# Attention and FFT gate on one core: matmuls in column and row tiles, the output projection one batch later, time in nine blocks

## The chip, the cores and the metric

The program runs on one core of a Trainium2 chip. A core has a matrix engine (PE in the profile, with its weight loads shown as PEld), a vector engine (DVE), a scalar engine (ACT), GpSimd (POOL) and a queue engine (SP). The engines run side by side, each takes its own instructions in order, and semaphores tie them together. Matmul results land in PSUM; everything else lives in SBUF. The metric is the device time of one execution in microseconds (us); the profile's span runs from the first to the last instruction.

## The reference

For 8 batches, 8 heads, 576 time steps and 64 channels per head, a linear attention without softmax is normalised per head, and its output (576 x 512 per batch) goes through a projection, a circular convolution in time, two gates and an output projection:

```python
kv = np.einsum('bhsd,bhse->bhde', k, v)
out = np.einsum('bhsd,bhde->bhse', q, kv)
rms = np.sqrt(np.mean(out * out, axis=-1, keepdims=True) + 1e-06)
x = out / rms * g_norm                      # then heads side by side: (B, 576, 512)
proj = x @ w_proj                           # 512 -> 3 * 512: x1, x2, x3
X2 = np.fft.rfft(x2, n=S, axis=1)
H = np.fft.rfft(filter_fft, n=S, axis=0)[None, :, :]
x2_conv = np.fft.irfft(X2 * H, n=S, axis=1)
y = x1 * x2_conv * x3
out = y @ w_out
```

All inputs and the output are float32 in memory; the kernel converts to bfloat16 as it loads and accumulates in float32.

## The kernel before

Channels lie on the partitions for most of the way (512 channels are four groups of 128, `NDC = 4`), time on the free axis. The Fourier transforms are matmuls with cosine and sine tables. Time is split in three thirds of 192 (`SB`): `fold` forms the sum of the thirds (`rr`) and two differences (`ab`). Frequencies that are multiples of 3 need only the sum (97 of them, group 0); the others need only the differences (group 1, and a mixed group for the last 64).

The start of the program (lines 59 to 174) builds the tables: six angle tables of 128 x 576, each with four DVE instructions (L158 to L162) and one sine on ACT (L163) into `IV`; the forward tables `FW` are 25 transposes of `IV` on PE (L173), copied out by DVE (L174). POOL issues all loads, which convert the type on the way: per batch four pieces of k, one of v, a remainder of each (`kt`, `vt`), and five of q (L107 to L115), then the weights `wp`, `wo` and the filter `fb`.

For each batch `b` the stages are these; tiles in PSUM come from one pool of four buffers of two banks each:

- `kv`: 20 matmuls of 128 x 128, of which only the two 64 x 64 blocks on the diagonal are kept (`kvblk`).
- `qtr`: q transposed with 20 transposes of 128 x 128, copied out by DVE in two instructions (L203).
- `att_o` (four calls): two matmuls of 288 columns; ACT writes the square and the scaled copy `osb`.
- `att_r`: sums of squares per head, eight matmuls of 288 columns onto 8 rows, then logarithm and exponential on ACT (`lr`, `rstd`).
- `att_x` (four calls): two matmuls (contraction over 8 rows) spread `rstd` over the channels, DVE multiplies into `x`.
- `fold`: three DVE instructions, `rr` and `ab`.
- `proj2`: 20 matmuls of 512 columns for x2; five row blocks of 128, two of them from `rr` (192 columns padded to 256).
- `fft`: 13 matmuls of 512 columns; DVE multiplies by the filter's transform (L302, L303, L308), POOL adds (L304) into `Y`.
- `proj13` (four calls): 16 matmuls of 288 columns for x1 and x3; ACT copies x1, DVE multiplies (`g13`).
- `invc` and `inv` (four calls): the inverse transform; `invc` gives the part that is the same in all three thirds (`cs`), `inv` the rest with four pairs of matmuls of 384 and 192 columns (L343, L345), then two DVE instructions (L347, L348) into `yg`.
- `outp`: 20 matmuls of 512 columns, four of them for the last 64 rows; ACT copies to `ot`, SP stores.

`gen_h` transforms the filter once, with 40 matmuls ahead of the first `proj2`. The loop over `b` runs `proj2(b)`, then `kv` and `qtr` of `b + 1`, `fft(b)`, the loads for `b + 2`, `proj13(b)` with `att_o(b + 1)` in turn, `invc(b)`, `att_r(b + 1)`, `inv(b)` with `att_x(b + 1)` in turn, `fold(b + 1)` and `outp(b)`. A planner at build time takes this order as priorities: an instruction that would not be ready can be passed by a later one of the same engine, and it chooses the PSUM buffer; the resulting order per engine is fixed. In the trace the PE keeps the written order, but for `outp`, whose tail rows are taken between the others.

Of the kernel before, what the change touches and what calls it, by code (L numbers as in the profile page):

```python
# [9 lines left out]
FP32 = mybir.dt.float32  # L10
# [5 lines left out]
P = 128  # L16
# [4 lines left out]
def kernel(  # L21
# [49 lines left out]

# [6 lines left out]
    ind_sq = consts.tile([P, 4, 8], BF16)  # L78
    nc.vector.memset(ind_sq, 0.0)
    for j in range(4):  # L80
        nc.vector.memset(ind_sq[0:64, j, 2 * j:2 * j + 1], 1.0)
        nc.vector.memset(ind_sq[64:128, j, 2 * j + 1:2 * j + 2], 1.0)
    ind_bc = consts.tile([8, 4, 2, 64], BF16)
    nc.vector.memset(ind_bc, 0.0)
    nc.gpsimd.affine_select(
        out=ind_bc, in_=ind_bc, compare_op=ALU.not_equal, fill=1.0,
        base=0, pattern=[[-2, 4], [-1, 2], [0, 64]], channel_multiplier=1)

    kb = [consts.tile([P, 4, H, D], BF16, name="kb%d" % i) for i in range(2)]
    vb = [consts.tile([P, H, 4, D], BF16, name="vb%d" % i) for i in range(2)]
    kt = [consts.tile([P, H, D], BF16, name="kt%d" % i) for i in range(2)]
    vt = [consts.tile([P, H, D], BF16, name="vt%d" % i) for i in range(2)]
    qb = [consts.tile([P, NSC, DM], BF16, name="qb%d" % i) for i in range(2)]
    for i in range(2):
        for t in (kt[i], vt[i], qb[i][:, 4]):
            nc.vector.memset(t[TAIL:P], 0.0)

    def load_kv(b):  # L100
        i = b % 2

        def src4(t, extra, ap):
            return bass.AP(tensor=t.tensor, offset=t.offset + b * H * S * D + extra, ap=[[4 * D, P], [S * D, H], ap])

        for c in range(4):
            nc.gpsimd.dma_start(out=kb[i][:, c], in_=src4(k, c * D, [1, D]))  # L107
        nc.gpsimd.dma_start(out=kt[i][:TAIL], in_=k[b, :, 4 * P:S, :].transpose([1, 0, 2]))
        nc.gpsimd.dma_start(out=vb[i].rearrange("p h c d -> p h (c d)"), in_=src4(v, 0, [1, 4 * D]))
        nc.gpsimd.dma_start(out=vt[i][:TAIL], in_=v[b, :, 4 * P:S, :].transpose([1, 0, 2]))  # L110

    def load_q(b):
        for c in range(NSC):
            n = min(P, S - c * P)
            nc.gpsimd.dma_start(out=qb[b % 2][:n, c], in_=q[b, :, c * P:c * P + n, :].transpose([1, 0, 2]))  # L115

    load_kv(0)
    load_q(0)

    fb = work.tile([P, NSC, DM], BF16, name="fb", tag="x2")  # L120
    wo = consts.tile([P, NDC, DM], BF16)
    wp = consts.tile([P, NDC, D3], BF16)

    def load_w(dst, src):
        nc.gpsimd.dma_start(out=dst, in_=src.rearrange("(c p) d -> p c d", p=P))

    load_w(wp[:, :, DM:2 * DM], moe_w_proj[:, DM:2 * DM])
    load_w(fb[:, 0:4], moe_filter_fft[0:4 * P, :])
    nc.gpsimd.dma_start(out=fb[:TAIL, 4], in_=moe_filter_fft[4 * P:S, :])
    nc.vector.memset(fb[TAIL:P, 4], 0.0)  # L130
    for part in (0, 2):
        load_w(wp[:, :, part * DM:(part + 1) * DM], moe_w_proj[:, part * DM:(part + 1) * DM])
    load_w(wo, moe_w_out)

# [3 lines left out]
    rr = [consts.tile([P, NDC, 256], BF16, name="rr%d" % i) for i in range(2)]  # L138
    for i in range(2):
        nc.vector.memset(kvblk[i], 0.0)  # L140
        nc.vector.memset(rr[i][:, :, SB:256], 0.0)


    nc.vector.tensor_copy(out=kcol, in_=ki)
    Q4 = float(S // 4)
    nc.vector.memset(phase, 0.0)
    nc.vector.memset(phase[:, 0:1], Q4)
    nc.vector.memset(phase[:, 2:3], Q4)
    nc.vector.memset(phase[0:64, 4:5], Q4)
    nc.vector.memset(phase[64:128, 5:6], -Q4)  # L150
    tv = work.tile([P, S], FP32, name="tv", tag="g13")
    nc.vector.tensor_copy(out=tv, in_=tvi)

    IV = consts.tile([P, 6, S], BF16)
    for c in range(6):
        ang = work.tile([P, S], FP32, name="ang", tag="tpw", bufs=2)
        rnd = work.tile([P, S], FP32, name="rnd", tag="ot", bufs=3)
        nc.vector.tensor_scalar(out=ang, in0=tv, scalar1=kcol[:, c:c + 1], scalar2=phase[:, c:c + 1],  # L158
# [275 lines left out]
```

## Time and profile before

| quantity | value |
|---|---|
| median of three runs | 299.29 us (299.08 to 299.79) |
| the profiled execution itself | 299.9 us |
| its span | 297.9 us |
| mean granted clock of the matrix engine | 0.986 |
| instructions | 4540 |

The profile gives busy time by engine, by line and by shape, and it can give each engine's instructions in order of time. Starts are the surest thing in it for the PE: matmuls overlap in the pipeline and their ends are modelled, so a stage is measured here from the start of its first matmul to the start of the next stage's first.

### The profile page before, as it was taken

The page shows a single profiled execution, that of the slowest core. Times are in us where ns is not written, and L with a number is a line of the kernel's source. Part 1 is how long each engine was busy: PE and PEld are TensorE (multiplying, and loading weights), DVE is VectorE, ACT ScalarE, POOL GpSimd, SP SyncE. Part 2 cuts the span into 40 slices and gives each one's busy share as a digit, 9 for nine tenths or more (in the row PEclk, how much of TensorE's full clock was granted, in tenths as well). Part 3 has the DMA queues.
Part 4 walks back from the last instruction along what each step waited for, and adds up shares of the span by engine and source line. Part 5 has one row for each costly group of instructions (what it writes and reads, how often), then busy time and mean ns, then how long its engine had stood idle before and what let it go on. Part 6 is the DMA issues. An engine that isn't in the chain of part 4 may idle for free.

```text
span 297.9 us, 4540 instructions
## 1 busy us (share of the span) xinstructions
PE 260.5 (87%) x1816; PEld 158.6 (53%) x1833; DVE 175.0 (59%) x272; ACT 131.6 (44%) x197; POOL 124.2 (42%) x131
## 2 busy tenths in 40 slices
PE   0128699999999999999999999999999999999992
PEld 0027346664567436754666455744775367644760
DVE  7993431939184745657383909382756547482760
ACT  1135435380637243753457073815274336614313
POOL 8874568890099006920395019800240006000600
PEclk9999779999999999999999999999999999999999
DMA  5999999999499639990699049934000220004004
GB/s 34 151 189 206 172 126 152 112 104 71 161 87 112 42 134 79 124 64 27 150 144 78 2 158 115 105 21 161 0 3 0 81 80 0 3 0 158 2 0 158
DMA packets 95415, 26.58 MB, mean 89 GB/s; under 512 B 79970, under 2 KB 90786, under 8 KB 95394
## 3 DMA queue, kind: packets, MB, share of 16 engines
q0 software_dynamic: 90272, 16.85, 69.3%
q1 hardware_dynamic: 5122, 9.44, 8.9%
q8 instruction: 14, 0.23, 0.3%
q14 instruction: 7, 0.06, 0.1%
HBM read 33.69 MB, written 9.44 MB: 145 GB/s over the span
## 4 chain that ended last, share of the span: by engine, by line
PE 66%; DVE 19%; ACT 10%; issue 4%; ACTq 0%; DVEq 0%
PE ps_x L319 17%; PE ps_out L359 12%; PE ps_x L286 12%; PE ps_inv L343 6%; DVE tpw L302 5%; PE ps_bc L234 4%; DVE qT L203 3%; DVE tpw L303 3%; PE ps_kv L186 3%; PE ps_inv L345 2%; ACT osb L214 2%; PE ps_h L262 2%; ACT sq L213 2%; PE ps_qT L202 2%; PE ps_o L212 2%
## 5 line engine op out<-in xcount | busy, mean ns | idle before, releaser
L319 PE MATMUL ps_x<-x,wp 128*128 128x288 bf16 x512 | 67.5, 286 | 4.4 <-DVE tpw L303 4.4
L304 POOL TENSOR_TENSOR Y<-tpw 97x1024 bf16<-97x1024 f32 (+1 forms) x16 | 38.0, 2381 | 74.8 <-DVE tpw L303 74.8
L319 PEld LDWEIGHTS <-wp 128*128 128x128 bf16 x512 | 50.0, 98 | 19.7 <-issue 5.7
L107 POOL DMA_DIRECT2D kb<-in_k_dram x32 | 28.5, 903 | 73.3 <-PE ps_kv L187 67.3
L361 ACT COPY ot<-ps_out 128x1024 f32<-128x1024 f32 (+1 forms) x24 | 20.0, 867 | 63.7 <-PE ps_out L359 63.1
L203 DVE COPY qT<-ps_qT 128x1152 bf16<-128x1152 bf16 x16 | 11.5, 753 | 52.3 <-PE ps_qT L202 52.3
L325 DVE TENSOR_TENSOR g<-ps_x,x 128x576 bf16<-128x576 f32 x32 | 24.0, 754 | 25.7 <-PE ps_x L319 25.7
L359 PE MATMUL ps_out<-wo,yg 128*128 128x512 bf16 (+1 forms) x152 | 38.2, 383 | 0.4
L323 ACT CAST x<-ps_x 128x576 bf16<-128x576 f32 x32 | 20.4, 639 | 39.7 <-PE ps_x L319 39.7
L115 POOL DMA_DIRECT2D qb<-in_q_dram x40 | 34.0, 879 | 2.1 <-DMA wo<-in_moe_w_out_dram 1.8
L347 DVE TENSOR_TENSOR u<-ps_inv,cs 128x576 bf16<-128x576 f32 x32 | 24.0, 753 | 17.0 <-PE ps_inv L345 17.0
L343 PE MATMUL ps_inv<-IV,Y 128*128 128x384 bf16 x128 | 34.0, 328 | 0.0
L345 PE MATMUL ps_inv<-IV,Y 128*128 128x192 bf16 x128 | 31.4, 246 | 0.0
L235 DVE TENSOR_TENSOR x<-ps_bc,osb 128x576 bf16<-128x576 f32 x32 | 23.7, 749 | 7.1 <-PE ps_bc L234 6.2
L213 ACT ACTIVATE sq<-ps_o 128x576 bf16<-128x576 f32 x32 | 20.9, 652 | 15.4 <-PE ps_o L212 15.4
L359 PEld LDWEIGHTS <-yg 128*128 128x128 bf16 (+1 forms) x160 | 14.0, 100 | 23.9 <-issue 8.4
L288 ACT CAST x<-ps_x 128x1024 bf16<-128x1024 f32 (+1 forms) x24 | 20.1, 872 | 11.2 <-PE ps_x L286 11.2
L214 ACT ACTIVATE osb<-ps_o,g_col 128x576 bf16<-128x576 f32 x32 | 23.6, 738 | 0.0
L302 DVE TENSOR_TENSOR tpw<-ps_X,HH 97x1024 f32<-97x1024 f32 (+1 forms) x16 | 19.5, 1219 | 6.8 <-PE ps_X L300 6.3
L286 PE MATMUL ps_x<-wp,ab 128*128 128x512 bf16 x96 | 22.0, 379 | 0.0
L173 PE MATMUL ps_ft<-ident,IV 128*128 128x128 bf16 (+1 forms) x25 | 3.7, 306 | 18.9 <-ACT IV L163 18.3
L343 PEld LDWEIGHTS <-Y 128*128 128x128 bf16 x128 | 12.5, 97 | 13.1 <-issue 6.7
(91 smaller groups left out, 355.0 us busy)
## 6 DMA issues: line engine op xcount, KB each, us to landing
out_dram<-ot SPq DMA_DIRECT2D x16, 512.0 KB, 3.1
kb<-in_k_dram POOLq DMA_DIRECT2D x32, 128.0 KB, 4.6
vb<-in_v_dram POOLq DMA_DIRECT2D x8, 512.0 KB, 6.8
qb<-in_q_dram POOLq DMA_DIRECT2D x32, 128.0 KB, 5.8
wp<-in_moe_w_proj_dram POOLq DMA_DIRECT2D x3, 512.0 KB, 10.5
out_dram<-ot SPq DMA_DIRECT2D x8, 128.0 KB, 3.1
kt<-in_k_dram POOLq DMA_DIRECT2D x8, 64.0 KB, 4.0
vt<-in_v_dram POOLq DMA_DIRECT2D x8, 64.0 KB, 5.8
```

What stands on the lines that cost most here:

```text
L107: nc.gpsimd.dma_start(out=kb[i][:, c], in_=src4(k, c * D, [1, D]))
L115: nc.gpsimd.dma_start(out=qb[b % 2][:n, c], in_=q[b, :, c * P:c * P + n, :].transpose([1, 0, 2]))
L213: nc.scalar.activation(out=s['sq'][:, j].rearrange("p (a b) -> p a b", a=2), in_=op[:, :, 0:TH], func=AF.Square)
L214: nc.scalar.activation(out=s['o'][:, j].rearrange("p (a b) -> p a b", a=2), in_=op[:, :, 0:TH], func=AF.Copy, scale=g_col)
L286: nc.tensor.matmul(pp[:, cc], t[:, j, o * P:(o + 1) * P], wp[:, j, DM:2 * DM], start=(j == 0), stop=(j == NDC - 1))
L302: nc.vector.tensor_mul(out=t_[:n, 0], in0=xp[:n], in1=HH[:n, g, 1:3])
L304: nc.gpsimd.tensor_add(out=Y[:n, 2 * g:2 * g + 2], in0=t_[:n, :, 0], in1=t_[:n, :, 1])
L319: nc.tensor.matmul(pp[:, h, 0:TH], w_, x[:, j, h * TH:(h + 1) * TH], start=(j == 0), stop=(j == NDC - 1))
L325: nc.vector.tensor_mul(out=st[b]['g13'][:, dc].rearrange("p (a b) -> p a b", a=2), in0=pp[:, :, 0:TH], in1=x1)
L343: nc.tensor.matmul(ip[:, 0:2, 0:SB], Y[:, g, d_], IV[:, g, 0:2 * SB].rearrange("p (a b) -> p a b", a=2), start=(g == 2), stop=(g == 5))
L345: nc.tensor.matmul(ip[:, 2, 0:SB], Y[:, g, d_], IV[:, g, 2 * SB:S], start=(g == 2), stop=(g == 5))
L359: nc.tensor.matmul(pp[:m, cc], yg[:, dc, c * P:c * P + m], wo[:, dc], start=(dc == 0), stop=(dc == NDC - 1))
```

## The change

The three thirds of time are each divided further by the remainder modulo 3: t = 192 m + 3 p + c with m, c in 0..2 and p in 0..63, so nine blocks of 64, block index 3 m + c. q is loaded in that order (three neighbouring rows are one piece of 192 numbers), the tables use it, and the output rows are stored from it with a stride of three rows, 64 partitions to a transfer. k is loaded as v is, four rows in one piece. Per batch, POOL issues six loads where there were thirteen.

Matmuls that used part of the matrix array are placed in column or row tiles: in `kv` each head has its own 64 x 64 product (40 matmuls of 64 columns, two column halves in turn); `qtr` has 36 transposes of 64 input columns (two halves in turn, four DVE copies); `att_r` writes four groups of 32 rows; `att_x` contracts over four groups of 32 rows, two at a time into two PSUM tiles; `proj2` computes the 64 rows left of `rr` as two halves of the contraction, which `fft` adds through a doubled table `FWr`; the last 64 output rows of two neighbouring batches are computed together.

`inv` computes two of the three thirds for a pair of channel groups and takes the last as the common part minus the others. `outp` runs one batch later, between `att_r` and `att_x`; `fold` comes before `invc`. The tables are built from three angle sets with the absolute value and two sines each. The filter is loaded as float32 by SP, folded by DVE (`fold_filter`) and transformed with 22 matmuls. The loads of batch 1 are issued right behind the weights; in the first batch the scaled copy `osb` is made by DVE.

```diff
+    def load_kv(b):
+        for i, src in enumerate((k, v)):
+            nc.gpsimd.dma_start(
+                out=kvm[b % 2][i].rearrange("p h c d -> p h (c d)"),
+                in_=bass.AP(tensor=src.tensor, offset=src.offset + b * H * S * D,
+                            ap=[[4 * D, P], [S * D, H], [1, 4 * D]]))
+            nc.gpsimd.dma_start(out=kvt[b % 2][i][:TAIL], in_=src[b, :, 4 * P:S, :].transpose([1, 0, 2]))
+    def load_q(b):
+        for g in range(2):
+            nc.gpsimd.dma_start(
+                out=qb[b % 2][64 * g:64 * g + 64].rearrange("p h (m x) -> p (h m) x", m=3),
+                in_=bass.AP(tensor=q.tensor, offset=q.offset + (b * H + 4 * g) * S * D,
+                            ap=[[3 * D, 64], [SB * D, 12], [1, 3 * D]]))
...
+    for c, tag in enumerate(("x", "Y", "g13")):
+        ang = work.tile([P, 2, S], FP32, name="ang", tag=tag)
+        a_, r_ = ang[:, 0], ang[:, 1]
+        nc.vector.tensor_scalar_mul(out=a_, in0=tv, scalar1=kcol[:, c:c + 1])
+        nc.vector.tensor_scalar(out=r_, in0=a_, scalar1=1.0 / S, scalar2=MAGIC, op0=ALU.mult, op1=ALU.add)
+        nc.vector.tensor_scalar(out=r_, in0=r_, scalar1=MAGIC, scalar2=-float(S), op0=ALU.subtract, op1=ALU.mult)
+        nc.vector.tensor_tensor(out=r_, in0=r_, in1=a_, op=ALU.add)
+        nc.scalar.activation(out=a_, in_=r_, func=AF.Abs)
...
+            nc.scalar.activation(out=IV[:, 2 * c + 1], in_=r_, func=AF.Sin, scale=W0)
+            nc.scalar.activation(out=IV[:, 2 * c], in_=a_, func=AF.Sin, scale=-W0, bias=half_pi[:, 0:1])
...
     def kv(b):
+        for j in range(NDC):
+            for c in range(NSC):
+                for hp in range(2):
+                    h = 2 * j + hp
+                    kk, vv = (km[:, h, c], vm[:, h, c]) if c < 4 else (kt[:, h], vt[:, h])
+                    nc.tensor.matmul(kvp[64 * hp:64 * hp + 64, 0, j * D:(j + 1) * D], kk, vv,
+                                     start=(c == 0), stop=(c == NSC - 1))
...
     def qtr(b):
+            for bank, cs in ((0, range(0, 4)), (1, range(4, NR))):
+                for i, c in enumerate(cs):
+                    for hp in range(2):
+                        nc.tensor.transpose(tp[64 * hp:64 * hp + 64, bank, i * P:(i + 1) * P],
+                                            qb[b % 2][:, 2 * jj + hp, c * D:(c + 1) * D], ident)
...
     def att_r(b):
+        for h in range(2):
+            for j in range(NDC):
+                nc.tensor.matmul(r2[32 * j:32 * j + 32, h, 0:TH], ind_sq, s['sq'][:, j, h * TH:(h + 1) * TH], start=True, stop=True)
...
+    def att_x(b, jp):
+        bc = [ps_tile("ps_bc") for _ in range(2)]
         for h in range(2):
+            for i in range(2):
+                r = slice(32 * (2 * jp + i), 32 * (2 * jp + i) + 32)
+                nc.tensor.matmul(bc[i][:, h, 0:TH], ind_bc[r], s['rstd'][r, h], start=True, stop=True)
...
+    def fold_filter():
+        nc.vector.tensor_add(out=t0[:, 0], in0=fa[:, 0], in1=fa[:, 1])
+        nc.vector.tensor_add(out=ff[:, 0], in0=t0[:, 0], in1=fa[:, 2])
+        nc.vector.tensor_add(out=t0[0:64, 1], in0=fc[0:64, 0], in1=fc[0:64, 1])
+        nc.vector.tensor_add(out=ff[0:64, 1], in0=t0[0:64, 1], in1=fa[0:64, 3])
+        nc.vector.tensor_sub(out=ff[:, 2], in0=fa[:, 0], in1=fa[:, 2])
+        nc.vector.tensor_sub(out=ff[:, 3:5], in0=fc2[:, :, 0], in1=fc2[:, :, 1])
...
     def proj2(b):
+        for j in range(NDC):
+            nc.tensor.matmul(pp[:, 0], rr[:, j, 0:P], wp[:, j, DM:2 * DM], start=(j == 0), stop=(j == NDC - 1))
+        for j in range(2):
+            for i in range(2):
+                nc.tensor.matmul(pp[64 * i:64 * i + 64, 1], rr[:, 2 * i + j, P:SB], wp[:, 2 * i + j, DM:2 * DM],
+                                 start=(j == 0), stop=(j == 1))
...
+    def inv(b, dp):
+        for i in range(2):
+            d_ = slice((2 * dp + i) * P, (2 * dp + i + 1) * P)
+            for g in range(2, 6):
+                nc.tensor.matmul(ip[:, i, 0:2 * SB], Y[:, g, d_], IV[:, g, 0:2 * SB], start=(g == 2), stop=(g == 5))
...
+        nc.vector.tensor_add(out=u[:, :, 0:2], in0=pq, in1=cs.to_broadcast([P, 2, 2, SB]))
+        nc.vector.tensor_sub(out=w_, in0=cs[:, :, 0], in1=pq[:, :, 0])
+        nc.vector.tensor_sub(out=u[:, :, 2], in0=w_, in1=pq[:, :, 1])
+        nc.vector.tensor_mul(out=st[b]['yg'][:, d2], in0=u.rearrange("p i m r -> p i (m r)"), in1=g13[:, d2])
...
     def outp(b):
+            if c0 == 4 and b % 2 == 0:
+                continue
...
+                for dc in range(NDC):
+                    for i in range(2):
+                        nc.tensor.matmul(pp[64 * i:64 * i + 64, 0], yt[i][:, dc, 4 * P:S], wo[:, dc],
+                                         start=(dc == 0), stop=(dc == NDC - 1))
...
+            for i in range(2):
+                eng = nc.scalar if b == B - 1 and i else nc.sync
...
-        invc(b)
         if nxt:
             att_r(b + 1)
-        for dc in range(NDC):
-            inv(b, dc)
-            if nxt:
-                att_x(b + 1, dc)
+        if b:
+            outp(b - 1)
+            del st[b - 1]
         if nxt:
+            att_x(b + 1, 0)
+            att_x(b + 1, 1)
             fold(b + 1)
-        outp(b)
-        del st[b]
+        invc(b)
+        for dp in range(2):
+            inv(b, dp)
+    outp(B - 1)
```

Of the two halves of a shared tail block, `yt[0]` and `yt[1]` are the `yg` of an even batch and of the odd one behind it. With `yg` in three buffers, a batch's gated result can wait for its projection.

332 lines of the change are left out of this document (165 added, 167 removed).

## The prediction
> **What bounds the kernel now.** I read the page first, engine shares before anything else.
>
> ```profile
> PE 260.5 (87%) x1816; PEld 158.6 (53%) x1833; DVE 175.0 (59%) x272; ACT 131.6 (44%) x197; POOL 124.2 (42%) x131
> ```
>
> PE is busy 87% of the span, the next engine 59%. A share is an average, so the second view is the stretches of one batch in the steady loop, cut where each stage's first matmul starts. Columns: from:to, length, then busy time of each engine.
>
> ```profile
> 108.44:112.77 4.33, 4.33 (x22) 1.97 (x22) 0.00 (x0) 2.94 (x4) 0.00 (x0) 1.00 0.79 276
> 112.77:113.88 1.11, 1.11 (x21) 1.11 (x20) 0.00 (x0) 0.83 (x2) 0.00 (x0) 1.00 0.00 0
> 113.88:115.00 1.12, 1.12 (x24) 1.12 (x21) 0.36 (x1) 0.73 (x2) 0.88 (x2) 1.00 0.00 0
> 115.00:117.81 2.81, 2.76 (x16) 1.36 (x15) 2.74 (x4) 0.00 (x0) 2.81 (x5) 1.00 1.12 72
> 117.81:119.77 1.96, 1.96 (x18) 1.57 (x17) 1.96 (x3) 0.64 (x1) 1.96 (x3) 1.00 2.17 138
> 119.77:127.41 7.64, 7.01 (x58) 5.47 (x56) 4.29 (x5) 5.54 (x9) 7.64 (x7) 1.00 1.27 114
> 127.41:128.17 0.76, 0.76 (x10) 0.60 (x8) 0.73 (x1) 0.56 (x2) 0.76 (x2) 1.00 1.89 120
> 128.17:129.25 1.08, 1.08 (x10) 0.62 (x9) 0.03 (x1) 1.08 (x3) 0.58 (x1) 1.00 1.56 111
> 129.25:135.58 6.33, 5.78 (x41) 3.11 (x40) 4.95 (x9) 1.62 (x3) 0.00 (x0) 1.00 0.59 37
> 135.58:140.35 4.77, 4.72 (x21) 1.76 (x21) 3.88 (x8) 1.24 (x2) 0.00 (x0) 1.00 0.00 0
> ```
>
> In order: `proj2`, `kv`, `qtr`, `fft`, the first `proj13`, the rest of `proj13` with `att_o`, `invc`, `att_r`, `inv` with `att_x`, `outp`. They add up to 31.91 us, and PE is busy in nearly all of it; the one long gap (7.64 against 7.01) lies in the sixth row. DMA (last two figures) is at zero in three stretches. So the loop is bound by columns streamed through PE. The counts in brackets include stragglers of the neighbours; with the code's counts the rates are 4.33/20 = 0.2165 us for 512 columns, 1.96/16 = 0.1225 for 288, 1.12/20 = 0.056 for 128. The rest of the run is the start and the end.
>
> ```profile
> 0.00:22.58 22.58, 3.67 (x26) 2.31 (x26) 20.95 (x60) 5.72 (x8) 18.86 (x33) 1.00 1.34 126
> 22.58:35.24 12.66, 8.99 (x65) 6.59 (x65) 3.65 (x7) 7.73 (x13) 5.74 (x7) 0.94 1.61 190
> 35.24:44.62 9.38, 9.16 (x41) 4.09 (x41) 4.91 (x8) 2.46 (x4) 6.57 (x9) 0.71 1.87 138
> 268.00:283.03 15.03, 14.98 (x98) 9.61 (x98) 7.83 (x8) 6.32 (x9) 4.68 (x2) 1.00 0.22 80
> 283.03:291.94 8.91, 8.86 (x60) 5.20 (x59) 5.17 (x9) 1.83 (x3) 0.00 (x0) 1.00 0.00 0
> 291.94:297.90 5.96, 0.49 (x2) 0.01 (x1) 0.00 (x0) 1.47 (x2) 0.00 (x0) 0.89 0.56 198
> ```
>
> These are the tables (DVE 20.95 of 22.58), attention of batch 0, `gen_h` (clock 0.71), then in the last batch `proj2` to `proj13`, inverse transform and output, and copy and store. Start 44.6 + 7 batches of 31.91 + 29.9 make the span.
>
> **A change of array shape costs 0.10 us.** PE in order of time:
>
> ```profile
> 130.95 0.40 PE L234 MATMUL ps_bc<-rstd,ind_bc 8*128 8x288 bf16 x2 [0.55 <-ACT rstd L226]
> 131.29 0.34 PE L343 MATMUL ps_inv<-IV,Y 128*128 128x384 bf16 x1
> 131.46 0.25 PE L345 MATMUL ps_inv<-IV,Y 128*128 128x192 bf16 x1
> 131.54 0.33 PE L343 MATMUL ps_inv<-IV,Y 128*128 128x384 bf16 x1
> ```
>
> Two matmuls of 288 columns should take 0.245; the next shape starts after 0.34. A pair 384 + 192 takes 0.25, of which 0.08 (0.76 - 0.10 over eight in `invc`) is the 192, so 0.165 remains for 384.
>
> **Do tiles run side by side?** One group of before does so: `gen_h` writes each column half in turn.
>
> ```profile
> L272 PE MATMUL ps_h<-fb,FW 128*64 128x512 bf16 x20 | 2.3, 381 | 0.0
> ...
> L272 PEld LDWEIGHTS <-FW 128*64 128x64 bf16 x20 | 1.0, 110 | 1.2 <-issue 0.4
> ```
>
> Twenty took 2.3 us, 0.115 each against 0.2165 alone: two halves run at once. No row shows it with 64 columns, with different moving data in the halves, or with row tiles. There I take overlap, and keep "none" as the other bound.
>
> **The loop after, on PE** (us per batch; bound without overlap in brackets):
>
> - `proj2`: 16 full and 4 half matmuls, 18 x 0.2165 + two shape changes = 4.10 (4.53).
> - `kv`: 40 of 64 columns, 40 x 0.028 = 1.12, as dear as now; if pairs overlap fully 0.56, if each costs as much as 128 columns 2.24. I take the middle, since each needs its own weight load.
> - `qtr`: 18 pairs x 0.056 = 1.00 (2.02). Two shape changes around both, 0.20.
> - `fft` 2.81 as now. `proj13` and `att_o`: 72 x 0.1225 = 8.82.
> - `att_r`: 2 x 0.1225 + 0.20 = 0.45 (1.18). `att_x`: 4 x 0.1225 + 0.20 = 0.69 (1.18); it loses the alternation with `inv`, eight shape changes.
> - `invc` 0.66; `inv` 16 x 0.165 = 2.64 for today's 3.9: 16 matmuls of 192 columns are gone.
> - `outp`: 16 x 0.2165 = 3.46. Every second batch the shared tail, 4 pairs + 0.20 = 1.07 (1.93).
>
> Sum 25.95, with the tail block 27.02. POOL has six load issues for thirteen ahead of its additions, SP four to six stores for three. Both run beside PE's 26 us and I charge nothing: POOL was busy 14.6 of 31.9 (the last bracketed column), and stores of 64 partitions have a whole batch before their `ot` buffer is needed. Without that cover a late store would hold ACT's next copy, and PE by way of PSUM.
>
> **What is late next: DVE.** Its instructions of one batch:
>
> ```profile
> L347 DVE TENSOR_TENSOR u<-ps_inv,cs 128x576 bf16<-128x576 f32 x4 | 3.0, 753 | 2.3 <-PE ps_inv L345 2.3
> L235 DVE TENSOR_TENSOR x<-ps_bc,osb 128x576 bf16<-128x576 f32 x4 | 3.0, 749 | 0.1
> L348 DVE TENSOR_TENSOR yg<-u,g 128x576 bf16<-128x576 bf16 x4 | 1.8, 446 | 0.0
> L203 DVE COPY qT<-ps_qT 128x1152 bf16<-128x1152 bf16 x2 | 1.4, 752 | 7.1 <-PE ps_qT L202 7.1
> L302 DVE TENSOR_TENSOR tpw<-ps_X,HH 97x1024 f32<-97x1024 f32 x1 | 1.2, 1224 | 0.1
> ...
> L246 DVE TENSOR_TENSOR ab<-x 128x1536 bf16<-128x1536 bf16 x1 | 0.9, 948 | 0.0
> L244 DVE TENSOR_TENSOR x<-x 128x768 bf16<-128x768 bf16 x1 | 0.5, 548 | 0.0
> ```
>
> From 576 and 1024 elements, a float32 operation costs 0.15 + 1.05 per thousand; from 576 and 768 in bf16, 0.14 + 0.53. `inv` per pair of groups: 768 elements 0.96, twice 384 at 0.555, 1152 bf16 at 0.75: 2.82, twice 5.6 for today's 4.8. `qtr` has two instructions more: +0.28. If 64-element runs halved the copy's rate, another 1.2; the rows show no such loss. DVE goes from 18.9 to 20.0 of some 27 us.
>
> That is less than PE, but it is bunched. From the first `att_x` matmul until the second `fft` tile is released, DVE must do 3.0 (x) + 2.05 (fold) + 5.6 + 1.78 + 4.86 (four of L302's kind) = 17.3 without a pause; successive instructions overlap (in the last two rows of the loop 9.85 of durations, L347, L235, L348 and the fold, make 4.95 + 3.88 = 8.83 busy: 0.07 for each of 15), so 23 of them take 15.7, and 16.1 with the start. PE has 15.4 of work in the same stretch: 0.69 + 0.66 + 2.64 + 4.10 + 1.12 + 1.20 + 2.81 + 2.2 for the first `proj13` and `att_o`. The second `proj13` waits for that tile already; from the view of waits, total us, times, longest:
>
> ```profile
> PE ps_x L319 <- DVE tpw L303: 4.4, 7, 0.6
> ```
>
> The 0.6 becomes 0.7 to 1.1, since DVE also pauses for a late `qtr`. `proj2` behind `inv` can also wait for `fold`, up to 1.0, which `kv` may fill. `att_r`, now right behind the last `att_o`, waits for ACT:
>
> ```profile
> L214 ACT ACTIVATE osb<-ps_o,g_col 128x576 bf16<-128x576 f32 x4 | 2.9, 734 | 0.0
> L213 ACT ACTIVATE sq<-ps_o 128x576 bf16<-128x576 f32 x4 | 2.6, 650 | 2.0 <-PE ps_o L212 2.0
> ...
> L224 ACT ACTIVATE lr<-ps_r,bias_eps 8x576 f32<-8x576 f32 x1 | 0.7, 727 | 0.0
> L226 ACT ACTIVATE rstd<-lr 8x576 bf16<-8x576 f32 x1 | 0.7, 682 | 0.0
> ```
>
> `invc` (0.76) used to cover the square (0.65). Now `outp(b - 1)` queues behind `att_r` on PE, and `lr` and `rstd` on ACT, unless the planner slips `outp` ahead; `outp` then hides both. I put all waits of a batch at 1.65: 1.1 for the tile and some 0.55 for square and fold (0.35 to 2.9 in all).
>
> So 27.6 per batch, plus 1.07 in three batches. The first loop batch has no `outp`, but gains little: square, copy, `lr` and `rstd` take 2.8 behind the last `att_o`, `x` and fold 5.05, so `proj2(1)` starts 7.9 behind it, and so do later ones (0.45 + 3.46 + 0.69 + 0.66 + 2.64 = 7.9). Only the bunching is absent: 27.6 - 1.1 = 26.5.
>
> **The start.** One of the four DVE instructions of a table:
>
> ```profile
> L158 DVE TENSOR_SCALAR ang<-tv,kcol,phase 128x576 f32<-128x576 f32 x6 | 4.0, 699 | 0.0
> ```
>
> Twelve for 24, at 0.7 about 8.4 us for 16.8, and they no longer stand before `kv(0)`. Then loads bound the start: k, v and q of a batch are 1.77 MB as stored, 9.3 us at the 190 GB/s of the stretch 22.58 to 35.24. The first stretch moved 126 x 22.58 = 2.85 MB, 15 us' worth at that rate, so up to 7 us go to getting started: 16. Attention of batch 0 took 12.66; `osb` on DVE takes four times 0.73 off ACT: 9.7, so 25.7; the products still running then (1.4) and `fold` (2.05) make 29.1. `gen_h` streams 16 slots (22 matmuls, twelve paired) for 30: at its 0.31 per slot 5.0 us for 9.4. If `fold_filter` runs while DVE waits, `gen_h` is hidden; if it runs behind `fold`, half of its 4.7 (five operations of 512 float32 elements at 0.69, one of 1024 at 1.2) and `gen_h` come on top: 36.6. The 15 transposes of the tables (25 before) lie in PE's waits here. Also `qtr(1)` needs two batches and the weights, 5.64 MB or 29.7 us of loading, so it can't run before 35, as if `proj2(0)` began at 30. I take 32 (28.5 to 37).
>
> **The end.** 15.03 becomes 14.8; `outp(6)` is moved here, 3.46; `invc` 0.66; the last `inv` with DVE's eight operations 6.8 (1.5 until the first can start, 5.3 for them), and behind it half of the last projection, 2.6: 28.3, then 5.96 + 0.2 as now: 34.5. That is 4.6 more than before: the projection's cover in the loop is paid back once.
>
> **Sum:** 32 + 26.5 + 6 x 27.6 + 3 x 1.07 + 34.5 = 261.8 span. The profiled execution took 299.9, 2.0 over its span, and the median of the runs is 1.4 over that span; 261.8 + 1.4 = 263.2.
>
> **Rivals.**
>
> 1. Narrow weight loads pace `kv` and `qtr`. Twenty took 1.0 us of PEld in L272, 0.05 each: 76 x 0.05 = 3.8 for 2.12, +1.7 x 7: 275. For: they are one per matmul. Against: the `qtr` row has 20 full loads in 1.12 us, each overlapping the next. Chance 0.15. The Trainium skill (TensorEngine Tiling (Array Packing), Restrictions and Gotchas) says that column tiling excludes the fast weight load; from the load rule in TensorE: Matmul & The Clock Gate, LDWEIGHTS (columns / 1.2), an estimate is 53 ns for 64 columns, and by it the time would be 277. The trace's 0.05 agrees with it, but in L272 the matmuls set the pace, so it doesn't show that loads would.
> 2. The start stays long: the float32 filter, 1.18 MB on SP's queue, shares the DMA engines with q. At 190 GB/s it costs 6.2 us, so `fold` ends at 35.3, and with `gen_h` (5.0) behind it `proj2(0)` starts at 40 to 41: 272. For: DMA was busy throughout that stretch. Against: DVE's tables delay the filter past most of q. Chance 0.13.
> 3. The change doesn't do what it says and nothing overlaps: the brackets add 0.43 + 1.12 + 1.02 + 0.73 + 0.49 + 0.4 = 4.2 x 7: 292. Against: L272. Chance 0.06.
> 4. Slower: narrow loads run one after the other at their 110 ns. 76 x 0.11 = 8.4 for 2.12, +6.2 x 7: 307. It decides from 0.095 per load (36 us over 7 x 76, on top of 0.028). Against: 20 x 110 ns fitted into 1.0 us in L272. Chance 0.03.
>
> The forecast, tiles side by side with DVE as a second bound, has 0.62.
>
> **Range.** Low: 28.5 + 25 + 6 x 26.3 + 3.2 + 33.5 + 1.4 = 249.4. High: 37 + 28 + 6 x 29.3 + 3.2 + 35 + 1.4 = 280.4, with narrow loads and long waits. 250 to 280 leaves out rivals 3 and 4 and some of the forecast's rim. A measurement of this kernel can tell about 0.2% from no change; faster 0.95, same 0.01, slower 0.04 (rival 4 and a little unknown).
>
> **What would show it.** Right: `proj2` starts some 28 us apart; `kv` and `qtr` at about 1.1 and 1.0; `att_r` under 0.5; PE's longest loop wait still for L303's successor; `proj2(0)` near 32; the last `outp` waiting for DVE. Wrong: `kv` at 2 (rival 1) or 4.4 (rival 4); `fold_filter` behind `fold` and `proj2(0)` near 40 (rival 2); `att_r` above 1 (rival 3).

## The result, and the profile after

The changed kernel takes 279.42 us (median of 4 runs, 278.70 to 279.43) against 299.40 for the kernel before (299.08 to 299.79, run beside it): a ratio of 0.933, 95% interval 0.931 to 0.935. Forecast were 263.2, in a range of 250 to 280. The time fell by 20 us where 36 were forecast.

The first line of the page of the changed kernel, and its stretches, cut where a stage's first matmul starts (from:to, length, busy time of PE, PEld, DVE, ACT and POOL, granted clock, DMA share and GB/s):

```profile
PE 230.8 (83%) x1942; PEld 132.6 (48%) x1965; DVE 181.4 (65%) x283; ACT 133.6 (48%) x197; POOL 79.6 (29%) x80
```

```profile
152.74:156.96 4.22, 4.17 (x21) 1.55 (x22) 4.15 (x7) 1.77 (x2) 0.00 (x0) 1.00 0.02 4
156.96:157.61 0.65, 0.65 (x42) 0.65 (x42) 0.62 (x2) 0.65 (x2) 0.00 (x0) 1.00 0.00 0
157.61:161.81 4.20, 4.15 (x60) 2.36 (x54) 3.68 (x7) 0.82 (x3) 3.75 (x5) 1.00 0.49 48
161.81:171.51 9.70, 9.07 (x73) 6.94 (x71) 6.32 (x8) 6.18 (x10) 5.60 (x4) 1.00 1.37 164
171.51:176.75 5.24, 5.19 (x33) 1.98 (x34) 0.69 (x1) 4.49 (x6) 0.00 (x0) 1.00 0.02 6
176.75:178.01 1.26, 0.98 (x10) 0.39 (x9) 0.81 (x2) 0.69 (x2) 0.00 (x0) 1.00 0.95 195
178.01:178.68 0.67, 0.67 (x9) 0.67 (x9) 0.67 (x2) 0.00 (x0) 0.00 (x0) 1.00 1.01 342
178.68:181.94 3.26, 2.76 (x19) 1.47 (x17) 3.23 (x6) 0.80 (x1) 0.00 (x0) 1.00 0.74 246
239.35:254.17 14.82, 14.77 (x96) 9.27 (x98) 12.96 (x16) 5.06 (x7) 4.67 (x2) 1.00 0.00 1
59.04:62.46 3.42, 1.03 (x17) 0.60 (x17) 1.08 (x2) 1.82 (x3) 0.00 (x0) 1.00 0.20 23
62.46:65.87 3.41, 3.41 (x16) 2.03 (x14) 3.38 (x6) 0.80 (x1) 0.00 (x0) 0.50 0.02 5
260.42:263.84 3.42, 1.02 (x6) 0.39 (x5) 3.39 (x6) 0.00 (x0) 0.00 (x0) 1.00 0.48 167
263.84:267.26 3.42, 3.42 (x11) 0.87 (x10) 1.33 (x3) 0.00 (x0) 0.00 (x0) 0.50 0.00 0
```

The first eight rows are one batch of the loop (with a tail block): `proj2`, `kv`, `qtr` with `fft`, `proj13` with `att_o`, `att_r` with `outp`, `att_x`, `invc`, `inv`. Together 29.20 us, where the batches before took 31.91. The next is the last batch up to the end of `proj13`. The last four come in pairs: a stretch in which PE is busy for less than a third, and then 3.4 us at half the clock. PE's waits, in total, times, longest:

```profile
PE ps_x L379 <- DVE tpw L363: 4.4, 7, 0.6
PE ps_qT L226 <- DVE qT L229: 4.0, 1, 4.0
...
PE ps_bc L267 <- ACT ot L440: 2.7, 6, 0.7
PE ps_x L334 <- DVE rr L281: 2.6, 7, 0.5
PE ps_out L432 <- DVE yg L413: 2.4, 1, 2.4
```

PE's own order of time for the low clock and for the end:

```profile
60.94 0.43 PE L267 MATMUL ps_bc<-rstd,ind_bc 32*128 32x288 bf16 x8 [1.57 <-ACT rstd L257]
62.19 1.23 PE L392 MATMUL ps_c<-IV,Y 97*128 97x192 bf16 x8 [0.81 <-DVE x L270]
63.21 4.08 PE L404 MATMUL ps_inv<-IV,Y 128*128 128x384 bf16 x16
...
178.68 2.76 PE L404 MATMUL ps_inv<-IV,Y 128*128 128x384 bf16 x16
...
263.45 1.55 PE L432 MATMUL ps_out<-wo,yg 128*128 128x512 bf16 x4 [2.40 <-DVE yg L413]
...
266.35 3.19 PE L432 MATMUL ps_out<-wo,yg 128*128 128x512 bf16 x11
```

The same sixteen `inv` matmuls take 4.08 us where the clock is at half until 65.87, and 2.76 at full. DVE at the start shows why `qtr` waited 4.0 us:

```profile
21.23 0.69 DVE L294 TENSOR_TENSOR t<-fa 128x512 f32<-128x512 f32 x1 [7.66 <-DMA fa<-in_moe_filter_fft_dram]
21.84 0.75 DVE L229 COPY qT<-ps_qT 128x512 bf16<-128x512 bf16 x2
```

The first `qT` copy stood behind `fold_filter`'s first addition in DVE's queue, and that addition waited for the filter. In the start PE also ran at half rate: matmuls of 512 columns start 0.43 us apart there, where the loop before took 0.2165:

```profile
34.27 0.63 PE L315 MATMUL ps_h<-ff,FW 128*97 128x512 bf16 x1
34.70 0.63 PE L315 MATMUL ps_h<-ff,FWr 128*97 128x512 bf16 x1
```

The 1.00 in the clock column says nothing of this: the recorded clock of this execution begins at 38.56, where the rate doubles.

To compare kernels I use one marker, the start of the first of the twelve `ab` matmuls of each `proj2` (1.52 us behind the stage's start in the loop). In the changed kernel these come at 40.90, 68.63, 96.84, 126.05, 154.26, 183.46, 211.68 and 240.87: batches of 28.2, and 29.2 with a tail block. So the span of 277.6 is a start of 39.4, seven batches of 200.0 in all, and 38.3 from the last start on.

| | forecast | measured |
|---|---|---|
| start, to `proj2(0)` | 32 | 39.4 |
| seven batches | 195.3 | 200.0 |
| end, from `proj2(7)` | 34.5 | 38.3 |
| span | 261.8 | 277.6 |

### The profile page after: what moved, and what is told of

Read it like the earlier page. It is cut to its first block, busy times and chain, and to the rows that moved or that the text cites. A ratio compares the mean times of both kernels' runs of the same rounds, so it can differ in the third digit from the quotient of the medians.

```text
span 277.6 us, 4744 instructions
## 1 busy us (share of the span) xinstructions
PE 230.8 (83%) x1942; PEld 132.6 (48%) x1965; DVE 181.4 (65%) x283; ACT 133.6 (48%) x197; POOL 79.6 (29%) x80
## 4 chain that ended last, share of the span: by engine, by line
PE 68%; DVE 19%; issue 5%; DMA 3%; ACT 2%; ACTq 0%; SPq 0%; DVEq 0%
PE ps_x L379 22%; PE ps_out L432 10%; PE ps_x L346 8%; DVE x L270 6%; PE ps_X L360 6%; DMA fa<-in_moe_filter_fft_dram 3%; PE ps_qT L226 3%; DVE tpw L363 3%; PE ps_x L334 3%; PE ps_o L240 2%; PE ps_kv L211 2%; PE ps_inv L404 2%; PE ps_x L338 2%; PE ps_X L367 2%; PE ps_out L436 2%
## 5 line engine op out<-in xcount | busy, mean ns | idle before, releaser
L432 PE MATMUL ps_out<-wo,yg 128*128 128x512 bf16 x120 | 30.7, 389 | 2.8 <-DVE yg L413 2.4
L82 POOL DMA_DIRECT2D km<-in_k_dram x8 | 7.4, 924 | 82.9 <-PE ps_qT L226 78.0
L404 PE MATMUL ps_inv<-IV,Y 128*128 128x384 bf16 x128 | 23.4, 339 | 0.0
L229 DVE COPY qT<-ps_qT 128x512 bf16<-128x512 bf16 (+1 forms) x32 | 13.2, 452 | 12.4 <-PE ps_qT L226 11.9
L340 ACT CAST x<-ps_x 128x1024 bf16<-128x1024 f32 x8 | 8.1, 1015 | 27.1 <-PE ps_x L338 27.1
L432 PEld LDWEIGHTS <-yg 128*128 128x128 bf16 x128 | 11.5, 99 | 17.8 <-issue 3.0
L362 DVE TENSOR_TENSOR tpw<-ps_X,HH 97x1024 f32<-97x1024 f32 (+1 forms) x16 | 19.5, 1219 | 0.2
L363 DVE TENSOR_TENSOR tpw<-ps_X,HH 97x1024 f32<-97x1024 f32 (+1 forms) x16 | 19.4, 1213 | 0.0
L409 DVE TENSOR_TENSOR u<-ps_inv,cs 128x768 bf16<-128x768 f32 x16 | 15.2, 949 | 4.7 <-PE ps_inv L404 4.7
L360 PE MATMUL ps_X<-x,FW 128*128 128x512 bf16 (+1 forms) x57 | 17.9, 389 | 0.4
L226 PE MATMUL ps_qT<-ident,qb 128*64 128x128 bf16 x288 | 11.9, 232 | 6.3 <-DVE qT L229 4.0
```

Of the source, the lines that this page charges most:

```text
L360: nc.tensor.matmul(xp[:n, ri], FWr[:, ri, 0:n] if c == 1 else FW[:, a, 2 * g + ri, 0:n], x2[:, c], start=(a == 0), stop=(a == len(ks) - 1))
L363: nc.vector.tensor_mul(out=t_[:n, 1], in0=xp[:n], in1=HH[:n, g, 0:2])
L404: nc.tensor.matmul(ip[:, i, 0:2 * SB], Y[:, g, d_], IV[:, g, 0:2 * SB], start=(g == 2), stop=(g == 5))
L432: nc.tensor.matmul(pp[:, cc], yg[:, dc, c * P:(c + 1) * P], wo[:, dc], start=(dc == 0), stop=(dc == NDC - 1))
```

## The experiments

Each kernel is the changed one with the edit shown. Ratios are to the kernel before, as measured on the same chip; the changed kernel has 0.933. "Marker" is the first `ab` start.

### The start: DVE's queue, then the loads

```diff
     tables()
+    fold_filter()      # its six additions held in program order
...
     fold(0)
-    fold_filter()
```

> The six fold_filter operations are held behind the qT copies on DVE; nothing else is changed. Theory (DVE's queue head): in the changed kernel the first fold_filter operation stood ahead of the finished qT copy and waited 7.66 us for the filter, and PE waited 4.03 us for that copy. Without it the second half of qtr starts near 18 instead of 22.3, att_o is then held by kvblk on ACT (21.3), so attention comes 2.4 us earlier; if gen_h also fits ahead of fold, up to 7. Time 272.5 to 277. Rival (the loads bound the start, as the prediction's second rival has it: filter and q share the DMA engines): the filter lands no earlier, gen_h stays behind it, time 279 to 279.5, and only the place of the wait changes.

Ratio 0.932 (0.930 to 0.935): no change, which is the rival's time. The wait of `qtr` for its copy is gone, but PE's waits now show two others:

```profile
PE ps_qT L226 <- DMA qb<-in_q_dram: 4.4, 1, 4.4
...
PE ps_bc L267 <- DVE osb L244: 2.4, 1, 2.4
```

q landed 2.1 us later in this execution (`qtr` at 18.16 for 16.05), and the additions now stand ahead of the last `osb` product on DVE, so PE waits there. The marker is 40.41. The filter's operations cost on DVE wherever they stand; this run couldn't separate that from the loads.

```diff
-        nc.vector.tensor_add(out=t0[:, 0], ...)
+        nc.gpsimd.tensor_add(out=t0[:, 0], ...)      # and the other five
...
+    fold_filter()
+    load_q(1)
     kv(0)
```

> The six fold_filter operations run on POOL, ahead of the q load of batch 1, instead of on DVE; DVE's queue at the start holds only tables, qT, osb, x and fold. Theory (the start is long because DVE has the filter to fold between its other work and gen_h comes behind fold for lack of it): nothing on DVE waits for the filter, gen_h (5.0 us) is done in PE's waits for rstd, x and fold, and the first run of ab matmuls starts at 36 to 37 instead of 40.9; 274.5 to 276. Rival (the loads bound it: q lands anywhere between 16 and 23 and the filter as late): ab starts at 39 to 42, 278 to 280. Second rival (POOL's additions, 2.36 us for 1024 elements, are too slow and delay gen_h and the q of batch 1): ab at 41 or later, 280 or more.

Ratio 0.937 (0.934 to 0.940): no gain over the changed kernel, yet the marker moved as the theory had it, from 40.90 to 35.98. PE in order of time (start, length, idle time before in brackets):

```profile
39.19 0.32 PE L210 MATMUL ps_kv<-vm,km 128*64 128x64 bf16 x8 [0.45 <-DMA vm<-in_v_dram]
...
42.76 1.06 PE L225 MATMUL ps_qT<-ident,qb 128*64 128x128 bf16 x16 [2.50 <-DMA qb<-in_q_dram]
```

`kv(1)` waits for v until 39.19 and `qtr(1)` for q until 42.76: behind these waits PE runs 3.4 us at half clock (42.46 to 45.87); the first batch takes 32.66 for 27.73, and the 4.9 us are given back. What is late next is the loads of batch 1. Whether the bytes ahead of them or POOL's later issue of q set that, the next run tells.

```diff
-    load_w(wo, moe_w_out)
     load_kv(1)
...
     fold_filter()
     load_q(1)
+    load_w(wo, moe_w_out)
```

with the split of `outp` and the move of `outp(6)`, which are shown below:

> Four edits together: fold_filter on POOL; the load of wo behind the loads of batch 1; outp split around att_x; outp(6) behind the last inverse transform. Theory for the start (with the filter out of DVE's way, the loads of batch 1 bind: in the run with fold_filter on POOL, kv(1) waited until 39.2 and qtr(1) until 42.8, with the DMA engines busy throughout): wo's share, 0.5 MB as stored, 2.7 us at 190 GB/s, goes from ahead of them, so that kv(1) doesn't wait and qtr(1) waits until 40; the second run of ab matmuls starts near 66, for 68.6. Together with the split (1.3) and the end (4.8): 269 to 271. Rival (POOL issues the q load behind its additions, and that issue binds, not the bytes): qtr(1) stays at 42.8, 271.5 to 273.5.

Ratio 0.908 (0.902 to 0.915), 271.46 us:

```profile
38.76 0.32 PE L209 MATMUL ps_kv<-vm,km 128*64 128x64 bf16 x8
...
40.43 0.64 PE L224 MATMUL ps_qT<-ident,qb 128*64 128x128 bf16 x16 [0.85 <-ACT kvblk L213]
```

POOL issued q as late as before (31.45 for 31.53), but with `wo` out of the way `kv(1)` no longer waits and `qtr(1)` starts 2.3 us earlier, no longer for q. So the bytes bound it. Their landing says the same: q of batch 1 landed at 42.1 in the changed kernel, where POOL issued it at 21.55 and 27.11, and at 42.6 with the filter on POOL, where POOL issued it at 31.53; with `wo` behind it, at 40.3. The second marker is 64.93 for 68.63. The time is just above the theory's 269 to 271 and just below the rival's range, and the four runs lie between 270.3 and 274.3; what decides is `qtr(1)` at 40.43.

### The tiles: are two halves really at work at once?

```diff
-            for c in range(NSC):
-                for hp in range(2):
+            for hp in range(2):
+                for c in range(NSC):
```

(and the same in `qtr`)

> In kv and qtr the matmuls of one column half run one after the other and then those of the other half, instead of in turn; the same work otherwise. Forecast's theory (two halves in turn run side by side): kv goes from 0.65 to 1.1 or more and qtr from 1.23 to 2.1, 1.3 us in each of eight batches: 288 to 291. Rivals 1, 3 and 4 of the prediction (narrow loads set the pace, or nothing overlaps): no change, 279 to 280.

Ratio 0.937 (0.932 to 0.941), batches of 28.36 and 29.34: 0.14 us more each, a tenth of the forecast. That spoke against overlap, until the order of starts was read:

```profile
157.60 0.34 PE L211 MATMUL ps_kv<-vm,km 128*64 128x64 bf16 x7
157.74 0.20 PE L211 MATMUL ps_kv<-vt,kt 128*64 128x64 bf16 x1
157.77 0.20 PE L211 MATMUL ps_kv<-vm,km 128*64 128x64 bf16 x2
```

The program has four `km` matmuls, one `kt`, four `km`, one `kt`. The trace starts seven `km` ahead of the first `kt`, most of them in pairs 5 ns apart: matmuls of the other half start before older ones of this half, provided that PE's queue holds the written order, which the trace doesn't print. The run therefore didn't do what it was meant to. A stronger one leaves the second half of the array unused:

```diff
-                    nc.tensor.matmul(kvp[64 * hp:64 * hp + 64, 0, j * D:(j + 1) * D], kk, vv,
+                    nc.tensor.matmul(kvp[0:64, hp, j * D:(j + 1) * D], kk, vv,
...
-                for dc in range(NDC):
-                    for i in range(2):
+                for i in range(2):
+                    for dc in range(NDC):
```

(the second part in the tail block of `outp`; `gen_h`'s mixed group likewise)

> kv writes the even and the odd heads into one column half of the array (two banks of PSUM) in the same order as before; in gen_h's mixed group and in outp's tail block the matmuls of one column half come all ahead of those of the other (six and four of 512 columns). Same work otherwise. Theory A (tiles in different halves run side by side, also where a few of one half stand in a row, as the queue in front of the array sorts them): with one half alone kv takes 40 x 0.027 = 1.1 us or more for 0.65, the tail block 1.7 to 1.9 for 0.99, gen_h's mixed group 2.6 for 1.4: 0.45 x 8 + 0.8 x 4 + 1.2, 284 to 287. Theory B (no overlap is needed: a matmul that uses half of the columns streams faster by itself, at 17 ns for 64 columns and 115 for 512): all three stay, 279 to 280.

Ratio 0.950 (0.946 to 0.954):

```profile
160.99 0.44 PE L211 MATMUL ps_kv<-vm,km 128*64 128x64 bf16 x8
...
162.26 0.62 PE L226 MATMUL ps_qT<-ident,qb 128*64 128x128 bf16 x15
...
180.43 1.06 PE L436 MATMUL ps_out<-wo,yg 128*64 128x512 bf16 x8
181.42 0.57 PE L267 MATMUL ps_bc<-rstd,ind_bc 32*128 32x288 bf16 x6
```

`kv` with one half takes 1.27 us (160.99 to 162.26) for 0.65, and the batches are 0.63 longer. So the overlap is real, and worth a factor of two in `kv`. The tail block, four of 512 columns in one half and then four in the other, still takes 0.99: order within such a group doesn't matter, as theory A had for "a few in a row" and against its figures of 1.7 to 1.9.

### The loop: PE, DVE and the waits

```diff
-        nc.vector.tensor_sub(out=ab, in0=x3[:, :, 0:2, :], ...)
+        tc.keep_in_program_order(
+            nc.vector.tensor_sub(out=ab, in0=x3[:, :, 0:2, :], ...))
```

> In fold the sum rr is written before the differences ab. Theory (proj2 waits for the last of three fold instructions): PE's 0.5 to 0.6 us wait ahead of proj2 goes in each of seven batches, 3 to 4 us in all: 275.5 to 276.5. Rival (DVE has no slack from att_x to the second fft tile, 16 us without a pause): the wait of proj2 goes and the wait of the second proj13 for that tile grows by as much, 279.0 to 279.6.

Ratio 0.933 (0.931 to 0.936). It tells nothing of either theory: `ab` came behind `rr`, but the planner put the first `u` of `inv`, of the same 0.95 us, in its place, so `rr` was as late as before.

```diff
         if b:
-            outp(b - 1)
+            outp(b - 1, (0,))          # one pair of row blocks
         if nxt:
             att_x(b + 1, 0)
             att_x(b + 1, 1)
             fold(b + 1)
+        if b:
+            outp(b - 1, (2, 4))        # the rest
```

> Of outp(b - 1) one pair of row blocks stays ahead of att_x(b + 1) and the rest, 1.73 us and the tail block of every second batch, goes behind att_x on PE. Theory (DVE starts its bunch too late): DVE has 1.7 to 2.8 us more lead, so the waits of att_x, inv and proj2 (0.16 and 0.5 to 0.6) and of the second proj13 (0.63) go: 1.2 us in each of six batches, 271 to 273. Theory with DVE as the bound of the stretch only: the wait for rr goes, the tile's stays: 276. Rival (PE's waits are shape changes and rates, not DVE): no change, 279.

Ratio 0.926 (0.922 to 0.930). Batches are 27.95 and 29.04: 0.2 less, not 1.2. PE:

```profile
172.59 0.43 PE L267 MATMUL ps_bc<-rstd,ind_bc 32*128 32x288 bf16 x6 [0.36 <-ACT rstd L257]
173.50 0.40 PE L267 MATMUL ps_bc<-rstd,ind_bc 32*128 32x288 bf16 x2 [0.47 <-ACT ot L440]
```

The wait for `rr` is gone, as both theories of DVE had it, but half of `outp` is too little to cover `rstd`, and 0.36 comes back there. The tile's wait stays at 0.63. The seven batches gain 1.3 us. The rest of what this execution gained lies in the start (marker 39.71) and in the end (35.2 us behind the last marker for 36.8), where the code is the same: behind the last wait for `yg` the clock didn't fall this time. It is the fastest of the four, too (275.41, the others 277.75 to 277.98), so the edit itself is worth about the 1.3.

```diff
             kv(b + 1)
-            qtr(b + 1)
         fft(b)
+        if nxt:
+            qtr(b + 1)
```

> qtr(b + 1) comes behind fft(b) on PE, with proj13 around it, kv stays ahead of it. The second proj13 waits 0.63 us in every batch for the tile that DVE's second L363 frees. Theory A (that wait is a chain of its own: from the first fft tile on, four DVE products of 1.2 us against 4.0 us of PE work; what DVE did before does not matter): qtr's 1.2 us lie in the chain and the wait goes, 0.4 to 0.8 per batch with the shape changes saved, 274 to 276.5. Theory B (the prediction's: DVE is late from att_x on, without a pause until that tile): the wait stays or moves to att_o, which then waits for qT, 279 to 281.

Ratio 0.992 (0.989 to 0.995), 297.22 us: 18 us worse than the changed kernel, outside both forecasts. DVE, then PE:

```profile
168.10 1.23 DVE L362 TENSOR_TENSOR tpw<-ps_X,HH 97x1024 f32<-97x1024 f32 x1 [0.90 <-PE ps_X L360]
```

```profile
170.51 0.41 PE L226 MATMUL ps_qT<-ident,qb 128*64 128x128 bf16 x8 [0.23 <-DVE tpw L363]
172.77 1.66 PE L379 MATMUL ps_x<-x,wp 128*128 128x288 bf16 x11 [1.85 <-DVE tpw L363]
```

DVE is idle 0.90 us ahead of the first product, so it isn't late from `att_x` on. In the changed kernel it isn't either, for it waits for PE ahead of the second pair of `qT` copies:

```profile
159.23 0.89 DVE L229 COPY qT<-ps_qT 128x640 bf16<-128x640 bf16 x2 [0.43 <-PE ps_qT L226]
```

Theory B falls. The wait is a chain of its own, four products behind the first `fft` tile, but theory A's remedy was wrong. `fft`'s three tiles and `qtr`'s first fill the four PSUM buffers, and now even the first `proj13` has to wait for the second L363.

```diff
-            for g in range(2, 6):      # two thirds on PE, the last by DVE
+            for g in range(2, 6):      # all three on PE: 384 and 192 columns, two DVE instructions
```

> inv computes all three thirds on PE again (four pairs of 384 and 192 columns for each channel group, two DVE instructions), as before the change; everything else as changed. Theory (PE bounds the loop): 16 matmuls of 192 columns more, 0.08 each, 1.3 us per batch, less the wait for rr (0.5), as DVE has 0.8 us less to do: 285 to 290. Rival (DVE's bunch bounds the loop): what PE loses DVE gains, 279 to 281.

Ratio 0.944 (0.942 to 0.947). Batches are 0.9 and 0.65 longer, 6.0 us over seven; but the end is 2.9 shorter, since DVE has less to do between the last `inv` and `outp`: the wait of 2.4 for `yg` is gone, and the clock doesn't fall there. The time lies between the two forecasts. PE is the bound in the loop, and DVE in the end.

```diff
-        if b:
-            outp(b - 1)
...
+        outp(b)           # at the end of its own batch; inv and att_x in turn
```

> outp(b) stands at the end of its own batch again, and inv and att_x alternate, as before the change; att_r stays ahead of them. Theory (outp one batch later is PE's cover for square, lr and rstd, and for x, fold and the last yg): without it PE waits for rstd at att_x (up to 1.5), for the last yg ahead of outp and for rr ahead of proj2, 2 to 3 us in each of seven batches, and the end is about as before: 290 to 298. Rival (the order among these stages doesn't matter, PE is the bound and the planner fills in): 277 to 281; the end alone would then gain 3 us, since outp(6) no longer stands there.

Ratio 1.051 (1.047 to 1.056), 315.13 us, slower than the kernel before; batches of 33.6 and 34.6 mostly. Its waits, and two of its stretches:

```profile
PE ps_out L432 <- DVE yg L413: 13.8, 13, 2.4
...
PE ps_out L432 <- DVE x L270: 9.7, 7, 1.4
```

```profile
97.90:101.32 3.42, 1.97 (x11) 0.61 (x9) 3.42 (x6) 0.00 (x0) 0.00 (x0) 1.00 0.00 0
101.32:108.16 6.84, 5.96 (x16) 1.80 (x16) 4.42 (x8) 0.83 (x1) 0.00 (x0) 0.50 0.01 2
```

The waits are those expected, but the price is 5.4 us per batch instead of 2 to 3. They explain 18.5 us (23.5 less the 5.0 that the changed kernel spends on `rr` and `yg`). Much of the rest is the clock: between the first marker and PE's last matmul it is at half for 34.1 us, against 6.8 in the changed kernel, which costs PE up to 14 us. The edit also lets `inv` and `att_x` take turns; what that alone costs was not tried.

### The end

```diff
-        if b:
+        if b and nxt:
             outp(b - 1)
...
+    outp(B - 2)
     outp(B - 1)
```

> In the last batch outp(6) comes behind the inverse transform instead of ahead of it, so that PE has it to do while DVE works on the last yg. Theory (the end is proj13, then the inverse transform's DVE chain of 7 us, with nothing for PE): the 3.45 us of outp(6) that stood ahead of invc go into that chain, and the low clock of the last slices with it: 275.5 to 276.5. Rival (the clock stays at 0.7 to 0.8 behind the long tail and the stores wait in ACT's queue): 2 us at most, 277.4 to 278.

Ratio 0.917 (0.912 to 0.922), 273.96 us. From the last marker to the end of the span 32.0 us for 36.8, a gain of 4.8, more than either forecast:

```profile
256.10 7.17 PE L432 MATMUL ps_out<-wo,yg 128*128 128x512 bf16 x32
263.21 1.05 PE L436 MATMUL ps_out<-wo,yg 128*64 128x512 bf16 x8
```

PE never stops and the clock never falls: 32 matmuls in 7.1 us. About 1.5 of the 4.8 is the clock, which the wait of 2.4 for `yg` doesn't cost each time: with `rr` first and with `outp` split the code of the end is that of the changed kernel, with the same wait, but the clock stayed up and the end took 35.3 and 35.2 us. Against those the fill is worth 3.3. The other 1.7 us of this run lie ahead of the first marker, which is 39.16 here with the same code.

### The best version

The kernel of four edits (above) with one more:

```diff
             outp(b - 1, (0,))
+        invc(b)
         if nxt:
             att_x(b + 1, 0)
```

> As the kernel of four edits before, and invc(b) comes ahead of att_x(b + 1) on PE. Theory (what is left of the waits for ACT in the loop can be filled: att_x waited 0.35 us for rstd in each of six batches, as only half of outp stands ahead of it): invc's 0.67 us fill it, 2.1 us in all: 269 to 269.7. Rival (x and fold start later behind invc, and proj2 waits for rr again, or the copy of cs on ACT delays ot): 271 to 272.

Ratio 0.906 (0.902 to 0.910): the same as without it, as the rival had it, though by another wait. Waits of the loop:

```profile
PE ps_bc L265 <- ACT ot L438: 1.5, 6, 0.2
PE ps_bc L265 <- DVE x L268: 1.2, 6, 0.2
```

The wait for `rstd` went, a new one of 0.2 for a PSUM tile that `x` still reads came, and the batches are 0.06 shorter. So the kernel with the four edits is as good and simpler: 9% faster than before, 2.6% faster than the change (0.908 to 0.933).

## Why the prediction was right and wrong

**Right in sign and in the bound.** PE has 83% of the span, and more PE work makes the loop longer (`inv` on all three thirds, `kv` in one half). The time lies 0.6 us inside the end of the range, though, and all three terms of the sum were too low. Tiles run side by side. `kv` was put in the middle, at 1.12, since each matmul needs its own load; it is 0.65, near the full overlap of 0.56. This ends rivals 1, 3 and 4: loads of 0.05 each would have given 2. The fast weight load that column tiling excludes, by the Trainium skill (TensorEngine Tiling (Array Packing), Restrictions and Gotchas), didn't matter here: 40 loads and matmuls took 16 ns each, where the estimate had 53 per load.

**The start, 7.4 too low.** The step that failed is "if `fold_filter` runs while DVE waits, `gen_h` is hidden". It ran ahead of the `qT` copies in DVE's fixed order and itself waited 7.66 us; and part of `gen_h` came behind `fold`. Nor was `gen_h` as cheap as its 5.0: at the half rate of the start it took 6.3 us in the run where it ran in one piece (the additions behind `qT`: 32.57 to 38.88). What the start would take at full clock was not tried.

Rival 2's figures were nearly met: `fold` ended at 35.64 for 35.3, and the start is 39.4 for 40 to 41. Its cause, the filter's bytes, is half of it. The filter's first part landed at 21.1, but only what stood behind it in DVE's queue was late: with the additions on POOL it landed at 21.2, and `att_x` started at 27.62 for 29.82. With the filter on POOL the bytes of batch 1 do bind: of `qtr(1)` the forecast said "it can't run before 35"; it was 42.8, which is `proj2(0)` at 37.9 (4.22 + 0.65 earlier) and not 30. The forecast's 5.64 MB leave out the filter, 6.2 us by its own rival 2. Both limits were within 2 us of each other, and the waits at the second cost a stretch of half clock besides, so taking the first away alone gained nothing.

**The loop, 4.7 too low.** The first batch was put at 26.5 and took 27.7. PE waited 1.57 for `rstd` and 0.81 for `x`, as forecast, and then ran 3.4 us at half clock, which I had not counted. Each other batch is 0.57 too low. By stage, measured less forecast: `kv` -0.47, `proj2` +0.12, `qtr` with `fft` +0.19, `att_r` and `outp` +0.26 (the planner took `outp` matmuls between those of `att_r`, and `fft` matmuls between `qtr`'s: more changes of shape), `att_x` +0.57 and `inv` +0.62 (0.28 and 0.50 of it PE idle). The forecast had no wait of `att_x` for a PSUM tile: ACT still copies `outp`'s result out of it, 2.7 us in six batches. `proj13` with its tile's wait came to 9.70 for 8.82 + 1.1. The forecast's DVE bunch from `att_x` to the tile was wrong as a mechanism: the tile's wait was 4.4 us in seven batches in the changed kernel, with `outp` split, with `outp` in its own batch and with `inv` in full, however early DVE was done with `x`. PE's waits in the batch shown come to 1.41 (0.63, 0.28, 0.50) for the 1.65 allowed; that this is near is luck in part, for the tile's was put at 1.1 and `att_x`'s not at all.

**The end, 3.8 too low.** `proj13` (14.82 for 14.8) and `outp(6)` (3.45 for 3.46) were right. The last `outp` waits for DVE, as forecast, but behind the wait the clock halves: from 257.62 to the last matmul 12.5 us for 10.1. The two runs whose clock stayed up there (`rr` first, `outp` split) took 11.0, so 1.5 of the 2.4 is the clock. From there to the end it was 7.5 for 6.16, with ACT issuing half of the last stores between its copies (that the queue is the cause was not tried alone). "Paid back once" was right, and could have been avoided by putting `outp(6)` there.

**What stays open.** The first marker lies between 39.2 and 42.4 in nine kernels whose start has the same code or nearly so, with q landing between 16 and 23 us. Why q lands so differently was not tried, and it doesn't order the markers: q let `qtr` start at 19.53 in the run with the marker at 39.16, and at 16.05 in the changed kernel with 40.90.

## What to carry to other kernels

A stage moved one batch later is cover, and worth what it covers: count what stands in the waits of the last batch too, and leave it something to do there. A wait at the start may hide a second limit just behind it; look at when the next batch's loads land before pricing the first. In a queue of fixed order, an instruction that waits for a transfer must not stand ahead of one that PE needs.

## What the hardware showed

Matmuls of different column halves start out of the written order: seven of `km` ahead of an older `kt`. The Trainium skill (TensorE: Matmul & The Clock Gate, The mechanism) says that matmuls start and end strictly in order; by this trace that doesn't hold between column halves, if the queue kept the written order. The order in which the halves are written is almost free (0.14 us per batch).

A short gap can cost twice. Two stretches of 3.42 us in which PE was busy for 1.02 and 1.03 were each followed by 3.4 us at half clock, and one with 1.97 busy by 6.84. The Trainium skill (TensorE: Matmul & The Clock Gate, What's actually happening) gives a free-running window of 3413 ns; the length agrees with 3.42. In every trace here the recorded changes of the clock lie whole multiples of that apart (62.45 and 263.84 in the changed kernel: 201.39, which is 59 times 3.413). Its rule names an idle window, and here windows with 30 to 58% of work were enough. But the share of work alone doesn't decide. In the run with `rr` first the wait of 2.40 us for the last `yg` left 45% in its window, and the clock stayed up:

```profile
261.09:264.50 3.41, 1.54 (x10) 0.70 (x8) 3.03 (x5) 0.03 (x1) 0.00 (x0) 1.00 0.73 241
264.50:267.92 3.42, 2.84 (x14) 1.07 (x15) 2.25 (x4) 0.00 (x0) 0.00 (x0) 1.00 0.00 0
```

In the changed kernel that wait lay within one window (261.05 to 263.45 in 260.42 to 263.84) and cost about 1.5 us more behind it; here it crossed an edge (262.63 to 265.03, the edge at 264.50) and cost nothing more. The same wait, 2.40 or 2.41 us, stands at the end of eight of the traces: in five it lies within one window, and half clock followed; in three (`rr` first, `outp` split, `qtr` behind `fft`) it crosses an edge, and none followed. So the price of a gap also depends on where it falls. What else decides stays open.
